# An attention and feed-forward kernel on one core: casts of sums moved to GpSimd, the sums of w2 spread over more blocks, and the weights of q and k loaded by block

## The chip, the core and the metric

The kernel runs on one core of a Trainium2 chip. The core has a matrix engine (TensorE, PE in the profile; its weight loads are PEld), three engines for elementwise work (VectorE or DVE, ScalarE or ACT, GpSimd or POOL) and SyncE (SP), whose queue issues the DMA transfers. Each engine works through its own queue in order: an instruction that waits holds up all that stand behind it on that engine. The metric is the device time in microseconds. Before the change three runs gave 889.3, 886.95 and 889.46 us, median 889.3.

## The reference

For 2048 tokens of width D = 512:

```python
xn = _layernorm(x)
q, k, v = split(xn @ wqkv)            # 32 heads of 16
scores = q k^T * 16**-0.5, kept where 0 <= i - j < 256
s = (softmax(scores) @ v) @ wo
h = silu(xn @ w1) * (xn @ w3)         # F = 1792
g = silu(h @ w2)
out = x + s * g
```

## The kernel before

**Tiles and precision.** The tokens are cut into NT = 4 blocks t of 512, and the 32 heads into four groups g. A tile (t, g) is one block of one group; two units of attention make a tile, so there are 32 units n, eight for each t. A product of two float32 matrices is made of float16 parts: each operand is cut into a high half (the cast) and a low half (what the cast left), and three matmuls are added: high by high, low by high, high by low. So every operand of a matmul costs a cast and a subtraction on one of the elementwise engines.

**What PE does in order.** The order of PE's instructions is the order in which the program makes them (only PE is in ORDERED). On the other engines a scheduler chooses the order, after dependences and priorities; the tanh and the products that free a PSUM bank are marked urgent. A unit of attention is a series of small steps: maxima of the scores (L639 on PE, L653 on DVE), scores again with the maximum taken off (L719), mask (L726, DVE), exponential (L729, ACT), values (L747), and the end of a tile (L762 to L802, normalise): sums are turned over through DRAM, `rb` is the reciprocal broadcast, POOL multiplies `on` by it, and `cut` makes the two halves of `on` for the product with wo. Between the steps the program spreads pieces of other work, each with a cost: projections of q and k (project, L583), values (L553), the feed forward (L978, L1168, L1098), and the totals (total, L1206 to L1221). `later(n, f)` puts f into a queue that is worked off n steps on, so that an elementwise step is placed in the program well before its user.

**Feed forward.** F is cut into FB = 14 blocks f. gate_up(t, f) multiplies xn by 128 columns of w1 (part k = 0, then tanh on ACT, L993, and a product on DVE, L997) and of w3 (k = 1, then L1002 on DVE). For t = 0 the blocks go into w2 by down (L1168), and the halves of w1 and w3 are stored to DRAM (dW1, L984) for t = 1 to 3, which load them ready made (L820). For t = 1 to 3 two blocks make a pair j (seven pairs), and the product with w2 is folded: seven products of sums (fold_down_piece, L1098) stand for eight of halves. The sums on the side of h are made for each t by fold_first (L1040, L1041) and fold_second (sums L1062 to L1065 on POOL, the casts L1055 on ACT, what the casts leave L1057 on POOL). The sums on the side of w2 are made once, by fold_weights(j), in t = 1 with f = 1 to 7: two raw blocks are loaded (L931), scaled (L940, ACT), summed (L925, POOL), cast (L948, ACT), subtracted (L950, POOL) and stored to DRAM (dW2, L955); load_fold (L1079) reads them. At the end of a t, unfold (L1132 and the helper halves, L327) makes four accumulators from the seven products on POOL, 14 additions, and total makes silu of each, multiplies it into the product of the attention with wo (L1212) and adds x. The last total of all goes by columns (L1234 to L1245).

**Slots.** Nearly all these tiles live in 47 slots of 2 KB in each partition. `take` gives the one that has been free longest; `give(x, after=n)` returns it n steps later. A new tile waits on the chip until the last reader of the old tile in that slot is done.

**Weights of q and k.** `weights_qk's cut` makes float16 halves of a group's weights (whi, wlo: eight tiles that stay in SBUF for the whole kernel), which project uses for every t.

## Time and profile before

| | |
|---|---|
| runs | 889.3, 886.95, 889.46 us (median 889.3) |
| profiled execution, its own time | 890.93 us |
| its span | 889.2 us |
| mean granted TensorE clock | 0.969 |
| PE busy | 812.9 us (91%) |
| DVE, ACT, POOL busy | 629.3, 434.3, 384.1 us |

The profile tells of one execution. The span is the time from the first to the last instruction, in microseconds; the profiled execution's own time lies 1.7 us above it. "PE 812.9 (91%)" is the busy time and its share of the span. A line of a timeline has the start, the duration, the engine, the source line, the operation and its tiles (out<-in), how many were put together (x9), and in brackets the idle time of the engine ahead of it with the instruction that ended the idle time ("<-ACT pt L729": ACT's line 729, which wrote tile pt). A line of a group gives the busy time of all and the mean in nanoseconds of one, then the idle time ahead of them and what ended it. A table of stretches has for each stretch the busy time of PE, PEld, DVE, ACT and POOL with their counts, the granted clock, the busy share of the DMA and its GB/s.

### The profile page before, as it was taken

Reading aid. Unit: us, or ns where it says so; the run is one execution under the profiler, and the core shown is the slowest. Engines: PE = TensorE matmul, PEld = TensorE weight load, DVE = VectorE, ACT = ScalarE, POOL = GpSimd, SP = SyncE. Lnnn points to the kernel's source line nnn. Section 1 sums busy time; section 2 is a strip of 40 time slices with the busy share of each in tenths; the row PEclk is TensorE's granted clock in tenths of the full one; section 3 lists DMA queues with packets and bytes.
Section 4 is the critical chain, followed back from the end, with each engine's and each line's share of the span. In section 5 each row is a group of like instructions: output and inputs, shape, how many; then the busy total and the mean of one; then the engine's idle time right before and its main releaser. Section 6 shows DMA issues by size and latency. Waiting matters only on the chain.

```text
span 889.2 us, 24220 instructions
## 1 busy us (share of the span) xinstructions
PE 812.9 (91%) x9302; PEld 424.7 (48%) x9302; DVE 629.3 (71%) x2013; ACT 434.3 (49%) x655; POOL 384.1 (43%) x621
## 2 busy tenths in 40 slices
PE   8999988999889669999999999999999998989995
PEld 4444444444434234654446544466445543457472
DVE  8787886788767438757878788866777776664444
ACT  6899773636365545434443344444444243444511
POOL 2257353524278786113351635310434453441653
PEclk9999999999989779999999999999999998999997
DMA  9978354353465466743543454554444641443321
GB/s 284 267 246 253 114 150 117 114 144 96 121 171 140 149 186 161 219 133 104 173 118 101 137 139 127 140 161 114 126 102 116 184 112 39 118 138 117 110 54 48
DMA packets 113812, 125.42 MB, mean 141 GB/s; under 512 B 18656, under 2 KB 76320, under 8 KB 113696
## 3 DMA queue, kind: packets, MB, share of 16 engines
q1 hardware_dynamic: 113408, 123.35, 49.0%
q8 instruction: 73, 1.20, 0.6%
q10 hardware_dynamic: 288, 0.52, 0.2%
q14 instruction: 43, 0.35, 0.1%
HBM read 88.21 MB, written 31.33 MB: 134 GB/s over the span
## 4 chain that ended last, share of the span: by engine, by line
PE 53%; DVE 12%; POOL 11%; ACT 10%; DMA 6%; issue 5%; SPq 2%; ACTq 0%; POOLq 0%; DVEq 0%
PE m L978 17%; PE m L1098 8%; PE po L747 7%; PE m L1212 5%; PE m L583 4%; DVE junk L653 3%; PE s L719 3%; PE m L553 3%; DMA slot<-in_B_w_dram 3%; POOL slot L327 3%; ACT pt L729 2%; ACT slot L330 2%; POOL slot L1057 2%; PE s L639 2%; DVE s L726 2%
## 5 line engine op out<-in xcount | busy, mean ns | idle before, releaser
L978 PE MATMUL m<-XH,slot 128*128 128x512 f16 x896 | 272.8, 387 | 17.5 <-DVE slot L997 13.6
L729 ACT ACTIVATE pt<-s,es 128x1024 f32<-128x1024 f32 x152 | 167.3, 1110 | 152.7 <-DVE s L726 145.3
L978 PEld LDWEIGHTS <-slot 128*128 128x128 f16 x1344 | 126.3, 99 | 178.0 <-issue 38.1
L327 POOL TENSOR_TENSOR slot<-slot,slot 128x256 f16<-128x256 f32 (+1 forms) x162 | 108.2, 695 | 195.5 <-ACT slot L1011 60.5
L978 PE MATMUL m<-XL,slot 128*128 128x512 f16 x448 | 172.3, 385 | 0.0
L726 DVE TENSOR_TENSOR s<-s,MK 128x256 f32<-128x256 f32 (+2 forms) x280 | 119.3, 435 | 60.0 <-PE s L719 57.7
L653 DVE CUSTOM_DVE_ANT_0 junk<-s,MW 128x320 bf16<-128x320 f32 x276 | 134.0, 485 | 25.4 <-PE s L639 17.1
L1098 PE MATMUL m<-slot,slot 128*128 128x256 f16 x882 | 102.5, 273 | 1.4 <-DVE slot L596 1.1
L1098 PEld LDWEIGHTS <-slot 128*128 128x128 f16 x882 | 84.5, 98 | 18.2 <-issue 4.6
L653 DVE CUSTOM_DVE_ANT_0 junk<-po,MW 128x320 bf16<-128x320 f32 x172 | 83.6, 486 | 5.8 <-DVE mt L678 0.6
L1057 POOL TENSOR_TENSOR slot<-slot,slot 128x256 f16<-128x256 f32 x126 | 82.0, 679 | 0.0
L719 PE MATMUL s<-qa,KA 50*64 50x320 f16 (+3 forms) x1472 | 60.6, 263 | 22.9 <-ACT pt L729 18.6
L997 DVE SCALAR_TENSOR_TENSOR slot<-slot,m 128x512 f32<-128x512 f32 x56 | 38.4, 685 | 58.7 <-ACT slot L993 57.5
L747 PE MATMUL po<-pt,V 64*32 64x320 f32 (+4 forms) x2880 | 78.7, 347 | 0.0
L1055 ACT CAST slot<-slot 128x512 f16<-128x512 f32 x63 | 38.9, 617 | 64.1 <-DVE slot L1002 31.8
L719 PEld LDWEIGHTS <-KA 50*64 50x64 f16 x1472 | 32.0, 106 | 74.8 <-issue 52.7
L747 PEld LDWEIGHTS po<-pt,V 64*32 64x32 f32 x2880 | 52.0, 107 | 21.6 <-issue 1.5
L1062 POOL TENSOR_TENSOR slot<-slot,slot 128x256 f32<-128x256 f32 x21 | 15.3, 727 | 99.2 <-DVE slot L1002 99.2
L639 PE MATMUL s<-KA,qa 48*64 48x320 f16 (+3 forms) x824 | 46.2, 297 | 12.1 <-ACT pt L729 10.8
L1212 PE MATMUL m<-slot,slot 128*128 128x512 f16 x180 | 47.8, 415 | 7.9 <-ACT slot L801 7.3
L993 ACT ACTIVATE slot<-m,sgs 128x512 f32<-128x512 f32 x56 | 38.2, 682 | 28.2 <-PE m L978 28.2
L327 POOL TENSOR_TENSOR on<-on,rb 128x256 f32<-128x256 f32 x32 | 23.1, 741 | 59.3 <-DMA rb<-de 59.2
(184 smaller groups left out, 1212.4 us busy)
## 6 DMA issues: line engine op xcount, KB each, us to landing
slot<-dW SPq DMA_DIRECT2D x147, 256.0 KB
slot<-in_B_w_dram SPq DMA_DIRECT2D x56, 256.0 KB
slot<-in_A_x_dram SPq DMA_DIRECT2D x30, 256.0 KB
dW<-slot SPq DMA_DIRECT2D x28, 256.0 KB
KA<-dK SPq DMA_DIRECT2D x24, 288.0 KB
dW<-slot SPq DMA_DIRECT2D x49, 128.0 KB
qa<-dQ SPq DMA_DIRECT2D x32, 192.0 KB
dQ<-slot SPq DMA_DIRECT2D x16, 256.0 KB
```

What stands on the lines that cost most here:

```text
L327: op(out[:, c], a[:, c], b[:, c])
L639: nc.tensor.matmul(s[c:c + w, r, :n], qa[rows, 2 * p + a, ii * P + c:ii * P + c + w], ka[rows, 2 * p + a, e - n:e], start=True, stop=True)
L653: lasts["maximum"] = nc.vector.tensor_tensor_reduce(out=junk[:, :n], in0=s[:, r, :n], in1=mask, scale=1.0, scalar=NEG, op0=ALU.add, op1=AL ...
L719: nc.tensor.matmul(s[64 * h:64 * h + 64, r, o:o + 64 * n], ka[rows, 2 * p + a, 64 * (m + 4):64 * (m + 5)], qa[rows, 2 * p + a, 64 * (m + k ...
L726: nc.vector.tensor_add(v, v, MK[:, kind, of:of + n, :].unsqueeze(1).to_broadcast([P, 2 * len(which), n, 64]))
L729: nc.scalar.activation(pt, s, AF.Exp, scale=es)
L747: nc.tensor.matmul(cell["po"][32 * i:32 * i + 32, h, 64 * (m + k):64 * (m + k + n)], V[64 * h:64 * h + 64, (4 * t + m // 2) % VB, hd * VW: ...
L978: nc.tensor.matmul(cell[k], w[:, (a * NC + c) * P:(a * NC + c + 1) * P], b[:, c, :], start=c == 0 and i == 0, stop=c == NC - 1 and i == 2)
L1055: nc.scalar.copy(hi, view)
L1057: sub(lo[:, k], view[:, k], hi[:, k])
L1098: nc.tensor.matmul(ps, made[:, f:f + P], wj[:, 256 * b:256 * b + 256], start=j == j0 and n == 0, stop=j == j1 - 1 and n == 2)
L1212: nc.tensor.matmul(ps, O[t, g][:, a, tb], w[g], start=g == 0 and i == 0, stop=g == NG - 1 and i == 2)
```

## The change

1. **Slots and weights of q and k.** SLOTS goes from 47 to 55. The eight constant tiles of q's and k's weights are gone: cut writes both halves of one of them into a slot (WQ[t, g, k]); after t = 0's projection the slot is stored to DRAM (dWQ, eight stores of 256 KB, eight steps later) and given back; for t = 1 to 3 load_qk loads it again at the end of the unit before its use (24 loads of 256 KB).
2. **fold_weights in three parts.** The pairs are loaded with blocks f of FOLD_AT, their sums are made with block f + 1, and the four cuts come 6, 8, 10 and 12 steps after that block's second piece. The slots of the raw sums are returned 6 steps later rather than 4.
3. **fold_second.** The casts of the two sums (not of o itself) are made by GpSimd, in two halves each, ahead of each subtraction; these two cuts come 2 and 4 steps later rather than 1 and 2.
4. **normalise.** The cast of `on` is made by GpSimd in two halves rather than by ACT.
5. **unfold.** For the last t the 14 additions are made by VectorE.
6. **Stores of dW1** come 8 steps later rather than 2.

```diff
@@ -52,3 +52,3 @@
 VB = 10
-SLOTS = 47
+SLOTS = 55
 ORDERED = {ENGINE.PE}
@@ -56,2 +56,3 @@
 FOLDS = ((0, 4), (4, 7))
+FOLD_AT = (0, 1, 2, 4, 6, 8, 10)
 SEVEN = (0, 1, 3, 4, 5, 6, 2)
@@ -223,2 +224,3 @@
     dK = [dram.tile([P, TERMS, S], F16, name=f"dK{g}") for g in range(NG)]
+    dWQ = dram.tile([NG, 2, P, 2 * D], F16, name="dWQ")
     dW1 = dram.tile([FB, 2, P, 2 * NC * P], F16, name="dW1")
@@ -334,3 +336,4 @@
 
-    WQK = {}
+    WQ = {}
+    ES = {}
     SQ = {}
@@ -392,9 +395,6 @@
         def cut(ks=(1, 0)):
-            if "hi" not in cell:
-                cell["hi"] = const.tile([P, 2, NC, P], F16, name=f"whi{g}")
-                cell["lo"] = const.tile([P, 2, NC, P], F16, name=f"wlo{g}")
-            hi, lo = cell["hi"], cell["lo"]
             for k in ks:
                 raw = cell["raw"][k]
-                split(hi[:, k].rearrange("p c f -> p (c f)"), lo[:, k].rearrange("p c f -> p (c f)"), raw, cell["sw"])
+                WQ[0, g, k] = both = take(F16)
+                split(both[:, 0:D], both[:, D:], raw, cell["sw"])
                 give(raw)
@@ -405,3 +405,3 @@
             nc.vector.tensor_scalar(es, cell["p2"], cell["p2"], DH**-0.5 / QS**2, op0=ALU.mult, op1=ALU.mult)
-            WQK[g] = hi, lo, es
+            ES[g] = es
         return load, norm, scale, cut
@@ -576,3 +576,3 @@
             assert turned[t] == 4
-            hi, lo, _ = WQK[g]
+            w = WQ[t, g, k]
             xh, xl = X[t]
@@ -581,4 +581,4 @@
             for c, i in parts[n]:
-                a, b = ((hi, xh), (lo, xh), (hi, xl))[i]
-                nc.tensor.matmul(cell["pp"], a[:, k, c, :], b[:, c, :], start=(c, i) == parts[0][0],
+                a, b = ((0, xh), (1, xh), (0, xl))[i]
+                nc.tensor.matmul(cell["pp"], w[:, (a * NC + c) * P:(a * NC + c + 1) * P], b[:, c, :], start=(c, i) == parts[0][0],
                                  stop=(c, i) == parts[-1][-1])
@@ -586,2 +586,9 @@
                 return
+            if t == 0:
+                def store():
+                    nc.sync.dma_start(dWQ[g, k], w)
+                    give(w, after=4)
+                later(8, store)
+            else:
+                give(w)
             pp = cell["pp"]
@@ -607,2 +614,6 @@
 
+    def load_qk(t, g, k):
+        WQ[t, g, k] = w = take(F16)
+        nc.sync.dma_start(w, dWQ[g, k])
+
     def fetch(t, g):
@@ -699,3 +710,3 @@
 
-        es = WQK[g][2]
+        es = ES[g]
         cell = {}
@@ -800,3 +811,4 @@
             O[t, g] = o = made.rearrange("p (a q) -> p a q", a=2)
-            nc.scalar.copy(o[:, 0, :], on)
+            for c in (slice(0, 256), slice(256, 512)):
+                nc.gpsimd.tensor_copy(o[:, 0, c], on[:, c])
             halves(nc.gpsimd.tensor_sub, o[:, 1, :], on, o[:, 0, :])
@@ -921,16 +933,12 @@
 
-    def pool_parts(op, *calls):
-
-        for out, a, b in calls:
-            op(out, a, b)
-
     def fold_weights(j):
 
-        raws = [take(F32) for _ in range(2)]
-        for i, raw in enumerate(raws):
-            nc.sync.dma_start(raw, w2[(2 * j + i) * P:(2 * j + i + 1) * P, :])
-        e, o = raws
+        cell = {}
         l, r = slice(0, 256), slice(256, 512)
         sub = nc.gpsimd.tensor_sub
-        cell = {}
+
+        def load():
+            cell["raw"] = [take(F32) for _ in range(2)]
+            for i, raw in enumerate(cell["raw"]):
+                nc.sync.dma_start(raw, w2[(2 * j + i) * P:(2 * j + i + 1) * P, :])
 
@@ -938,7 +946,10 @@
             assert folded
-            for i, raw in enumerate(raws):
+            e, o = cell["raw"]
+            for i, raw in enumerate((e, o)):
                 nc.scalar.activation(raw, raw, AF.Copy, scale=fold_w[:, 2 * j + i:2 * j + i + 1])
             cell["z"] = z, y = [take(F32) for _ in range(2)]
-            pool_parts(sub, (z[:, l], e[:, r], e[:, l]), (z[:, r], o[:, r], z[:, l]),
-                       (y[:, l], o[:, r], e[:, r]), (y[:, r], o[:, l], z[:, r]))
+            sub(z[:, l], e[:, r], e[:, l])
+            sub(z[:, r], o[:, r], z[:, l])
+            sub(y[:, l], o[:, r], e[:, r])
+            sub(y[:, r], o[:, l], z[:, r])
 
@@ -950,3 +961,3 @@
                 sub(a[:, n + c:n + c + 256], raw[:, c:c + 256], a[:, c:c + 256])
-            give(raw, after=4)
+            give(raw, after=6)
 
@@ -958,7 +969,9 @@
             later(4, store)
-        later(4, sums)
-        later(6, lambda: cut(e, 256, (0,)))
-        later(7, lambda: cut(o, 512, (1, 2)))
-        later(9, lambda: cut(cell["z"][0], 512, (4, 5)))
-        later(11, lambda: cut(cell["z"][1], 512, (6, 3)))
+
+        def cuts():
+            e, o = cell["raw"]
+            z, y = cell["z"]
+            for n, work in enumerate(((e, 256, (0,)), (o, 512, (1, 2)), (z, 512, (4, 5)), (y, 512, (6, 3)))):
+                later(2 * n, lambda work=work: cut(*work))
+        return load, sums, cuts
 
@@ -985,3 +998,3 @@
                     give(w, after=4)
-                later(2, store)
+                later(8, store)
             else:
@@ -1054,4 +1067,7 @@
             hi, lo = (made[:, 512 * k:512 * k + 512].rearrange("p (e c q) -> p e c q", e=2, c=2) for k in range(2))
-            nc.scalar.copy(hi, view)
+            if raw is o:
+                nc.scalar.copy(hi, view)
             for k in range(2):
+                if raw is not o:
+                    nc.gpsimd.tensor_copy(hi[:, k], view[:, k])
                 sub(lo[:, k], view[:, k], hi[:, k])
@@ -1066,4 +1082,4 @@
         cut(o, oo, (1, 3), (e,))
-        later(1, lambda: cut(sums[0], z, (4, 5)))
-        later(2, lambda: cut(sums[1], y, (6, 2)))
+        later(2, lambda: cut(sums[0], z, (4, 5)))
+        later(4, lambda: cut(sums[1], y, (6, 2)))
 
@@ -1124,3 +1140,3 @@
         q = [QS7.pop((t, i)) for i in range(7)]
-        add = nc.gpsimd.tensor_add
+        add = nc.gpsimd.tensor_add if t < NT - 1 else nc.vector.tensor_add
         for b in range(4):
@@ -1251,2 +1267,3 @@
         late = []
+        cuts_at = []
         for t in range(NT):
@@ -1271,4 +1288,9 @@
 
-                    if t == 1 and 1 <= f <= FB // 2:
-                        pieces.append((0, lambda f=f: fold_weights(f - 1)))
+                    if t == 1 and f in FOLD_AT:
+                        work = fold_weights(FOLD_AT.index(f))
+                        pieces.append((0, work[0]))
+                        cuts_at.append((f + 1, work))
+                    for at, work in cuts_at:
+                        if t == 1 and f == at:
+                            pieces.append((0, work[1]))
                 if f == FB - 4 and t + 2 < NT:
@@ -1278,3 +1300,7 @@
                     pieces += soon
-                pieces += gate_up(t, f)
+                made = gate_up(t, f)
+                for at, work in cuts_at:
+                    if t == 1 and f == at:
+                        made.insert(2, (0, lambda work=work: later(6, work[2])))
+                pieces += made
                 pieces += late
@@ -1485,2 +1511,3 @@
     beside = [[] for _ in units]
+    ahead = [[] for _ in units]
     for n in range(len(units)):
@@ -1488,6 +1515,7 @@
         for k in range(3, len(tiles)):
-            if max(2 * k - 5 + (k == NG), 0) == n:
-                beside[n] += project(*tiles[k], 1)
-            if 2 * k - 4 == n:
-                beside[n] += project(*tiles[k], 0)
+            for u, half in ((max(2 * k - 5 + (k == NG), 0), 1), (2 * k - 4, 0)):
+                if u == n:
+                    beside[n] += project(*tiles[k], half)
+                if u == n + 1 and tiles[k][0]:
+                    ahead[n].append((0, lambda k=k, half=half: load_qk(*tiles[k], half)))
         if n % 8 >= 4 and t < NT - 1:
@@ -1496,2 +1524,3 @@
             beside[n] += [(0, lambda t=t, b=n % 8 - 2: residual(t - 1, b))] + total(t - 1, n % 8 - 2)
+        beside[n] += ahead[n]
     other = [sum(c for c, _ in b) for b in beside]
```

## The prediction

> **What bounds the kernel now.** I read the head of the page first, then stretches of 25 us, then each idle time of TensorE (PE) of over half a microsecond, then on ScalarE (ACT) and GpSimd (POOL) what was late.
>
> ```profile
> span 889.2 us, 24220 instructions
> PE 812.9 (91%) x9302; PEld 424.7 (48%) x9302; DVE 629.3 (71%) x2013; ACT 434.3 (49%) x655; POOL 384.1 (43%) x621
> DMA packets 113812, 125.42 MB, mean 141 GB/s; under 512 B 18656, under 2 KB 76320, under 8 KB 113696
> ```
>
> PE is busy for 91%, and its order is fixed by the program. So the kernel shortens only where PE sits idle or runs at half clock. No other engine is full over the span, but the stretches differ (columns: start:end, length, busy us of each engine with its count, granted clock, DMA share, GB/s):
>
> ```profile
> 50.00:75.00 25.00, 23.50 (x186) 10.54 (x186) 20.08 (x79) 24.91 (x53) 16.10 (x26) 1.00 0.80 257
> 225.00:250.00 25.00, 21.03 (x274) 10.34 (x263) 20.30 (x66) 8.45 (x12) 9.20 (x14) 0.93 0.41 111
> 250.00:275.00 25.00, 20.73 (x233) 9.76 (x232) 14.86 (x51) 17.27 (x29) 21.72 (x34) 0.86 0.55 153
> 275.00:300.00 25.00, 17.62 (x225) 8.18 (x223) 12.61 (x37) 12.32 (x19) 20.88 (x33) 0.85 0.48 133
> 300.00:325.00 25.00, 16.57 (x120) 7.05 (x119) 9.51 (x32) 11.88 (x19) 19.04 (x30) 0.81 0.57 170
> 325.00:350.00 25.00, 23.59 (x290) 11.75 (x289) 18.93 (x57) 14.23 (x21) 15.84 (x25) 0.93 0.68 193
> 850.00:889.00 39.00, 27.88 (x190) 18.71 (x187) 17.80 (x24) 4.99 (x8) 19.55 (x27) 0.87 0.18 52
> ```
>
> From 225 to 350 PE is busy for 99.5 of 125 us, at clocks of 0.81 to 0.93. That is the stage in which w2's seven sums are made (fold_weights, seven times), and POOL is nearly full in its middle. The tail loses 11 us more. PE's idle times of that stage, of the later blocks and of the tail:
>
> ```profile
> 236.66 0.41 PE L719 MATMUL s<-qa,KA 50*64 50x320 f16 x9 [3.97 <-ACT pt L729]
> 263.60 1.01 PE L978 MATMUL m<-XH,slot 128*128 128x512 f16 x2 [4.27 <-DVE slot L997]
> 268.62 0.60 PE L978 MATMUL m<-XH,slot 128*128 128x512 f16 x2
> 297.79 1.01 PE L978 MATMUL m<-XH,slot 128*128 128x512 f16 x2 [7.38 <-DVE slot L997]
> 315.61 0.64 PE L719 MATMUL s<-qa,KA 50*64 50x320 f16 x12 [5.77 <-ACT pt L729]
> 324.78 0.33 PE L639 MATMUL s<-KA,qa 48*32 48x320 f16 x8 [2.65 <-ACT pt L729]
> 344.87 0.42 PE L719 MATMUL s<-qa,KA 50*64 50x320 f16 x11 [0.74 <-ACT pt L729]
> 437.08 0.42 PE L719 MATMUL s<-qa,KA 50*64 50x320 f16 x11 [2.07 <-ACT pt L729]
> 741.74 0.97 PE L719 MATMUL s<-qa,KA 50*64 50x320 f16 x24 [1.81 <-ACT pt L729]
> 743.95 0.48 PE L639 MATMUL po<-KA,qa 48*64 48x320 f16 x4 [1.23 <-DVE M L653]
> 842.77 0.59 PE L978 MATMUL m<-XH,slot 128*128 128x512 f16 x2 [1.03 <-DVE slot L997]
> 874.06 8.70 PE L1212 MATMUL m<-slot,slot 128*128 128x512 f16 x27 [7.31 <-ACT slot L801]
> ```
>
> After 263.60 two matmuls take 1.01 us, from 268.62 on 0.60: five microseconds after a long idle time run at some half speed, which costs about 2.4 us besides. I charge 2.4 us to each idle time of 4 us or more.
>
> Each of these waits ends at ACT, so the question is what held ACT. Ahead of 297.79 (ACT's timeline, then VectorE's, DVE):
>
> ```profile
> 291.41 0.62 ACT L1055 CAST slot<-slot 128x512 f16<-128x512 f32 x1 [1.49 <-POOL slot L1063]
> 293.97 0.62 ACT L948 CAST slot<-slot 128x512 f16<-128x512 f32 x1 [0.63 <-POOL slot L1057]
> 295.22 1.14 ACT L948 CAST slot<-slot 128x512 f16<-128x512 f32 x2 [0.63 <-POOL slot L1057]
> 296.26 0.68 ACT L993 ACTIVATE slot<-m,sgs 128x512 f32<-128x512 f32 x1
> ```
>
> ```profile
> 297.05 0.69 DVE L997 SCALAR_TENSOR_TENSOR slot<-slot,m 128x512 f32<-128x512 f32 x1 [8.65 <-ACT slot L993]
> ```
>
> The tanh (L993) that releases PE waits for nothing itself; it stands in ACT's queue behind casts whose inputs are sums that POOL has not made, or whose target slots POOL's subtractions still read. POOL is the resource of this stage, and ACT's first-in first-out queue carries its lateness to PE.
>
> **The change, part by part.** Prices of one instruction come from these groups:
>
> ```profile
> L1055 ACT CAST slot<-slot 128x512 f16<-128x512 f32 x63 | 38.9, 617 | 64.1 <-DVE slot L1002 31.8 <-POOL slot L1063 22.0 <-POOL slot L1065 10.1
> L801 ACT CAST slot<-on 128x512 f16<-128x512 f32 x16 | 9.9, 618 | 39.4 <-POOL on L327 36.6 <-DMA slot<-dW 2.8
> L1057 POOL TENSOR_TENSOR slot<-slot,slot 128x256 f16<-128x256 f32 x126 | 82.0, 679 | 0.0
> L1063 POOL TENSOR_TENSOR slot<-slot,slot 128x256 f32<-128x256 f32 x21 | 15.3, 729 | 1.4
> L1412 POOL MEMSET KA<- 128x384 f32 x4 | 1.5, 412 | 0.0
> L1244 DVE TENSOR_TENSOR slot<-slot,slot 128x256 f32<-128x256 f32 x2 | 0.8, 424 | 0.1
> ```
>
> POOL takes 84 half casts from fold_second (2 × 42 of the 63 casts of L1055) and 32 from normalise (2 × 16 of L801). The trace has no such copy. The memset of 384 columns at 0.412 us scales to 0.28 for 256 columns, the least; a two-input subtraction, 0.68, is the most. I take 0.42: one input, but it reads, so it lies between and nearer the memset. 116 × 0.42 = 49 us more on POOL (32 to 79), less 14 sums at 0.73 that leave: 384 becomes about 423 us. ACT loses 42 × 0.62 + 16 × 0.62 = 36 us. Neither total matters by itself; where they lie does.
>
> *w2's sums spread, casts off ACT.* Load, sums and cuts of the seven pairs go to blocks 0, 1, 2, 4, 6, 8, 10 and the blocks after. By the changed program's order, the stretch in which PE does what it did at 250 to 350 holds some 70 us of POOL work (added casts counted) against 82 before, and later stretches take the rest. Its first wait: at 229.27 the raw loads were issued, held behind a store,
>
> ```profile
> 221.94 0.35 SPq L955 DMA_DIRECT2D dW<-slot  x1
> 229.27 1.33 SPq L931 DMA_DIRECT2D slot<-in_B_w_dram  x3
> ```
>
> so ACT's scaling of them came late and PE stood at 236.66. Now the load stands a block ahead of the sums and that store comes later in SP's queue: −3.97 −2.4 = −6.4. At 263.60 the tanh now stands ahead of the casts of w2 that held it: −4.27 −2.4 = −6.7. The three from 315 to 345 were casts of L1055 waiting for L1063, now on POOL, and of a pair that is moved later: −5.77 −2.65 −0.74 −2.4 = −11.6.
>
> The wait of 297.79 does not go. In the new order, POOL gets from the place of 264.5 up to the sum that the last cast ahead of this tanh needs, some 52 instructions in a row: 9 copies × 0.42 + 15 sums × 0.73 + 27 subtractions × 0.68 = 33 us. It could start at 264.5, ends at 297.6 on before's clock; cast, tanh and product (0.62 + 0.68 + 0.69) bring PE to 299.6, while PE would be there at 297.79 − 7.38 = 290.4. So 9.2 us, and with short waits for DVE in between some 11.4, in place of 7.4: +4. Later, where two more pairs meet (the place of 404 to 413), a cast waits behind 8 us of POOL work with some 6 us of slack in ACT's queue: +2. Sum of the stage: −6.4 −6.7 −11.6 +4 +2 = −18.7. Bounds: all waits and half clocks gone, −34.5; copies at 0.68 and two stalls come back, +8.
>
> *Other blocks from t = 1 on.* 437.08, 741.74, 743.95 and 842.77 hold 2.07 + 1.81 + 1.23 + 1.03 = 6.1 us of waits, the first two and the last of the same kind. POOL's order there now does cast and subtraction in one go, and the later steps (2 and 4 for 1 and 2) leave the sums time. I take −5 (−9, if half as much again lies in shorter waits; or +3, if POOL, now fuller, delivers operands late).
>
> *Weights of q and k by block.* 8 stores and 24 loads of 256 KB more on SP, 32 issues at the 0.44 us of the three raw loads above = 14 us of SP's queue, and 8 MB on top of the 125 MB that the DMA moves. By the order each load stands at least 20 us of PE work ahead of its use. Nothing on the path; if that cover were gone, each of the 24 would be a wait like that of 236.66.
>
> *Later stores of w1 and w3* (8 steps for 2) and *55 slots*. In t = 0 SP now issues the loads of w1 and w3 at places some 4 us later against PE, and ACT is full there (24.91 of 25 at 50 to 75). PE has few waits there now. I take +2 for the stage (−3 with more slots free; +8 if half of the 14 blocks lose 1.1 us).
>
> *The tail.* The last unfold's 14 sums leave POOL for DVE:
>
> ```profile
> 858.34 3.78 SPq L795 DMA_DIRECT2D rb<-de  x8
> 867.87 1.86 POOL L327 TENSOR_TENSOR slot<-slot,slot 128x256 f32<-128x256 f32 x2
> 871.50 1.85 POOL L327 TENSOR_TENSOR on<-on,rb 128x256 f32<-128x256 f32 x2
> 873.39 0.62 ACT L801 CAST slot<-on 128x512 f16<-128x512 f32 x1 [1.18 <-POOL on L327]
> 867.92 2.35 DVE L1207 SCALAR_TENSOR_TENSOR slot<-slot,slot 128x512 f32<-128x512 f32 x2 [2.32 <-ACT slot L1206]
> ```
>
> The product with rb need no longer wait behind them. rb has landed by about 864 (its issues end at 862.1; I allow 2 us): two products 1.5, two copies 0.84, two subtractions 1.4, so PE may go on at 867.8 rather than 874.06: −6.2, and −2.4 as the idle time no longer reaches 4 us. DVE's remaining 8 sums × 0.42 end about 869, then the four products with tanh; it becomes the last, which gives some of that back: −7 (−4 to −8).
>
> Sum: −18.7 −5 +2 −7 = −28.7 against this execution's own 890.93, which is 1.6 above the median of 889.3: 862.
>
> **A rule against the change.** POOL's two sums at 867.87 took 1.86 us, where 2 × 0.73 would be 1.46, while DVE ran two L1207. The Trainium skill, "GPSIMD Engine Reference", section "1. Specifications", says that GpSimd shares its SBUF interfaces with VectorE and contends with DVE instructions that read two SBUF inputs. By that rule the casts belong on ACT; this row agrees. If every moved half cast were stretched by 1.86/1.46 as that row is, POOL gets 49 × 0.27 = 13 us more, a quarter of it in the crowded stage, so the sum would be near −25.
>
> **The rivals.** *POOL becomes the bound.* A copy costs 0.68 and the bunch at 264 to 287 has 9 × 0.26 = 2.3 us more, the stalls of 315 to 345 stay behind it (11.6 not gained), and the other blocks give nothing (5): 862 + 2.3 + 11.6 + 5 = 881. For it: POOL at 21 of 25 us already. Against: 12 us leave the stretch.
>
> *The stage is freed.* POOL's work shares out so that 297.79 goes too: −34.5 −5 +2 −7 gives 846. For it: less work than before; against: the 33 us in a row.
>
> *Slower: t = 0's loads of w1 and w3 come late.* The mechanism is SP's queue: stores of dW1 and dWQ and the loads of w1, w3 in one order, the latter issued 4 us later, at a DMA share of 0.80, and ACT with no slack to catch up. If each of the 14 blocks waits 3 us for its weights, +42 in place of +2: 862 + 40 = 902. It decides from 28.7 + 2 = 31 us, 2.2 us a block. Against: PE has 23.50 of 25 us there, and the loads still lead their use by 3.6 us and more.
>
> **How the numbers follow.** Forecast case (850 to 874) 0.50; freed (below 850) 0.10; POOL the bound (874 to 886.6) 0.18; within 0.3% of the median, about what the measurement can tell, 0.05; slower 0.17. So faster 0.78. The range: from the freed case's 846, less 1, to 892, with 0.17 above and 0.03 below; the forecast's own is 850 to 874.
>
> **What would show it.** PE's waits near 236 and 263 gone; one of 9 to 12 us on DVE's L1010 (L997 before) at some 285 to 300, with POOL full for 30 us ahead of it and ACT's cast of w2 before the tanh; no wait over 1 us where 315 to 345 was; POOL copies at 0.28 to 0.68; the last wait under 4 us. It is wrong if blocks of t = 0 wait for w1's loads, or if new waits on POOL stand in t = 2 and 3.

## The result and the profile after

The changed kernel takes 858.79 us (median of 856.75 to 859.68) against 889.38 for the kernel before: a ratio of 0.9651, with a 95% interval of 0.9616 to 0.9686. The forecast was 862. The head of the page of the changed kernel:

```profile
span 857.9 us, 24287 instructions
PE 804.5 (94%) x9302; PEld 420.7 (49%) x9302; DVE 635.0 (74%) x2027; ACT 402.1 (47%) x597; POOL 416.1 (49%) x723
```

POOL is 32 us busier and ACT 32 us less busy. PE's busy time fell by 8 us though its work is the same: fewer matmuls ran at half clock, and the mean granted clock rose from 0.969 to 0.982. The stage of w2's sums, in the same columns as before:

```profile
225.00:250.00 25.00, 23.23 (x306) 11.46 (x303) 22.57 (x73) 10.53 (x16) 15.19 (x25) 1.00 0.43 131
250.00:275.00 25.00, 22.92 (x274) 11.19 (x267) 16.37 (x50) 15.46 (x26) 20.35 (x34) 0.93 0.57 166
275.00:300.00 25.00, 13.97 (x180) 6.33 (x179) 10.28 (x31) 9.02 (x14) 24.62 (x41) 0.80 0.46 128
300.00:325.00 25.00, 24.86 (x275) 11.62 (x274) 20.13 (x64) 11.66 (x15) 9.16 (x16) 1.00 0.79 218
325.00:350.00 25.00, 25.00 (x325) 15.01 (x322) 19.49 (x65) 11.59 (x15) 15.14 (x25) 1.00 0.46 138
```

PE is busy for 110.0 us of the 125, where it was 99.5. What is left of the loss stands in one stretch, 275 to 300, in which POOL has 24.62 of 25 us. PE's waits of over 1.8 us from 200 to 600, and those of the tail:

```profile
265.43 0.41 PE L650 MATMUL po<-KA,qa 48*64 48x320 f16 x4 [1.89 <-DVE M L664]
296.12 1.01 PE L583 MATMUL m<-XH,slot 128*128 128x512 f16 x2 [11.03 <-DVE slot L1010]
398.10 0.42 PE L730 MATMUL s<-qa,KA 50*64 50x320 f16 x11 [2.34 <-ACT pt L740]
483.04 0.41 PE L730 MATMUL s<-qa,KA 50*64 50x320 f16 x8 [2.26 <-ACT pt L740]
537.82 0.59 PE L991 MATMUL m<-XH,slot 128*128 128x512 f16 x2 [2.09 <-DVE slot L1010]
845.09 2.98 PE L1228 MATMUL m<-slot,slot 128*128 128x512 f16 x13 [0.66 <-POOL slot L329]
848.71 2.75 PE L1228 MATMUL m<-slot,slot 128*128 128x512 f16 x12 [0.64 <-DVE slot L1232]
```

The waits of 236, 263, 315 and 324 are gone (the one of 265.43 is another's), that of 297 is longer (7.38 before), and the tail's 7.31 became two of 0.66 and 0.64.

PE's order is the same in all these kernels but for one piece, so each matmul of one trace can be lined up with the same matmul of another. The table has how far each kernel's profiled execution is behind (+) or ahead (−) of the kernel before's, at the place where the kernel before was at the time at the head of the column. It is worked out from the two traces and shows where time is won or lost. Each trace is one execution, and runs of one kernel differ by several us (e2_spread's from 880.9 to 891.2), so a difference of 2 or 3 us between two rows may be chance. The last column but one is the median of the runs, the last its ratio to the runs of the kernel before on the same chip. That kernel's median was 889.3 to 892.2 us from chip to chip, so two medians of different rows are comparable to some 2 us; the ratio is free of this.

| kernel | 225 | 350 | 425 | 575 | 650 | 775 | 850 | 875 | median | ratio [95%] |
|---|---|---|---|---|---|---|---|---|---|---|
| changed | +0.9 | −15.9 | −13.8 | −8.9 | −8.9 | −20.3 | −24.0 | −30.4 | 858.8 | 0.965 [0.962, 0.969] |
| e1_unfold | −0.8 | 0.0 | −1.2 | −2.0 | −2.0 | −5.6 | −3.8 | −7.6 | 885.8 | 0.994 [0.990, 0.999] |
| e2_spread | −0.4 | −8.3 | −4.0 | −0.3 | +0.2 | −2.3 | −0.4 | −0.4 | 886.6 | 0.996 [0.993, 0.999] |
| e3_casts | +1.5 | +9.4 | +7.3 | +5.3 | +5.7 | −0.9 | −1.6 | −0.6 | 889.0 | 0.997 [0.995, 1.000] |
| e4_slots | −0.2 | +5.2 | +4.6 | +6.6 | +6.4 | −0.2 | −2.7 | −2.7 | 886.8 | 0.996 [0.994, 0.998] |
| a1_casts_act | −0.1 | −14.2 | −14.2 | −4.0 | −4.0 | −10.0 | −12.4 | −19.7 | 870.0 | 0.976 [0.975, 0.978] |
| a5_nospread | +2.0 | +6.8 | +9.2 | +13.1 | +13.2 | +1.7 | −2.0 | −8.6 | 879.8 | 0.987 [0.984, 0.990] |
| a6_noslots | +2.4 | +1.0 | +3.4 | +0.9 | +1.0 | −5.8 | −4.3 | −10.6 | 879.2 | 0.986 [0.985, 0.988] |
| a7_s47 | +1.5 | −0.7 | +9.8 | +9.6 | +9.5 | +1.4 | +3.4 | −2.9 | 887.9 | 0.998 [0.996, 1.001] |
| a2_give8 | +3.4 | −10.4 | −6.5 | −3.0 | −3.2 | −11.7 | −15.4 | −22.0 | 867.3 | 0.976 [0.972, 0.979] |
| a3_w2_dve | +0.8 | −15.4 | −16.6 | −9.0 | −8.9 | −20.3 | −24.0 | −30.2 | 861.0 | 0.967 [0.964, 0.970] |
| a9_w2low_dve | +1.1 | −12.2 | −8.1 | −6.6 | −6.6 | −18.0 | −21.7 | −28.3 | 864.0 | 0.970 [0.965, 0.975] |
| a13_clear_queue | +0.7 | −7.2 | −7.7 | −1.0 | −0.9 | −14.0 | −17.7 | −23.9 | 869.3 | 0.976 [0.972, 0.980] |

Names with e are the kernel before with one part of the change, names with a the changed kernel with one thing undone or another one added.

### The profile page after: what moved, and what is told of

It is laid out like the page before. It is cut to its first block, busy times and chain, and to the rows that moved or that the text cites. A ratio compares the mean times of both kernels' runs of the same rounds, so it can differ in the third digit from the quotient of the medians.

```text
span 857.9 us, 24287 instructions
## 1 busy us (share of the span) xinstructions
PE 804.5 (94%) x9302; PEld 420.7 (49%) x9302; DVE 635.0 (74%) x2027; ACT 402.1 (47%) x597; POOL 416.1 (49%) x723
## 4 chain that ended last, share of the span: by engine, by line
PE 56%; DVE 14%; POOL 11%; DMA 6%; ACT 5%; issue 4%; SPq 2%; POOLq 0%; ACTq 0%; DVEq 0%
PE m L991 21%; PE m L1114 10%; PE po L758 6%; PE m L583 5%; DVE junk L664 4%; PE m L1228 4%; PE s L730 4%; DMA slot<-in_B_w_dram 3%; POOL slot L329 3%; PE m L553 2%; POOL slot L1073 2%; PE s L650 2%; PE m L1184 2%; DVE s L737 2%; ACT pt L740 1%
## 5 line engine op out<-in xcount | busy, mean ns | idle before, releaser
L991 PE MATMUL m<-XH,slot 128*128 128x512 f16 x896 | 272.9, 387 | 7.5 <-DVE slot L603 4.5
L991 PEld LDWEIGHTS <-slot 128*128 128x128 f16 x1344 | 126.2, 99 | 166.8 <-issue 28.3
L329 POOL TENSOR_TENSOR slot<-slot,slot 128x256 f16<-128x256 f32 (+1 forms) x156 | 104.2, 697 | 146.0 <-ACT slot L1024 68.2
L1114 PEld LDWEIGHTS <-slot 128*128 128x128 f16 x882 | 84.4, 98 | 19.1 <-issue 5.1
L583 PE MATMUL m<-XH,slot 128*128 128x512 f16 x240 | 72.4, 386 | 12.8 <-DVE slot L1010 12.8
L1073 POOL TENSOR_TENSOR slot<-slot,slot 128x256 f16<-128x256 f32 x126 | 82.7, 676 | 0.6
L583 PEld LDWEIGHTS <-slot 128*128 128x128 f16 x384 | 36.1, 99 | 56.7 <-issue 17.4
L1006 ACT ACTIVATE slot<-m,sgs 128x512 f32<-128x512 f32 x56 | 38.2, 682 | 37.9 <-PE m L991 37.8
```

What stands on the lines that cost most here:

```text
L329: op(out[:, c], a[:, c], b[:, c])
L583: nc.tensor.matmul(cell["pp"], w[:, (a * NC + c) * P:(a * NC + c + 1) * P], b[:, c, :], start=(c, i) == parts[0][0], stop=(c, i) == parts[ ...
L991: nc.tensor.matmul(cell[k], w[:, (a * NC + c) * P:(a * NC + c + 1) * P], b[:, c, :], start=c == 0 and i == 0, stop=c == NC - 1 and i == 2)
L1073: sub(lo[:, k], view[:, k], hi[:, k])
L1114: nc.tensor.matmul(ps, made[:, f:f + P], wj[:, 256 * b:256 * b + 256], start=j == j0 and n == 0, stop=j == j1 - 1 and n == 2)
```

## The experiments

**One part alone.** Four kernels took one part each.

e1_unfold, the last unfold on VectorE:

```diff
-        add = nc.gpsimd.tensor_add
+        add = nc.gpsimd.tensor_add if t < NT - 1 else nc.vector.tensor_add
```

> The kernel before with one part of the change: the last unfold's 14 additions on VectorE. If the tail gains because GpSimd no longer holds the product with rb back, as predicted: 4 to 8 us less than before, nothing moved ahead of 850 us, and the last wait of TensorE, 7.3 us before, under 2 us. Rival: the tail only follows from what happened ahead of it (GpSimd's backlog of the last folds), and the addition on VectorE delays the products with tanh there: under 2 us gained.

The median fell by 4.8 us, within what the first theory gave. The trace has 3.8 us of its 7.6 behind 850; the rest had wandered in before, which this edit doesn't touch. PE's last wait is 3.51 us, not under 2. So the edit alone is worth about 4 us in the tail, and the changed kernel gains about 7 there (−24.0 at 850, −31.3 at the end of the span). Three kernels that keep both this edit and the casts of `on` on GpSimd, and each lack another part, gain as much there (a1_casts_act 8.5, a5_nospread 7.3, a6_noslots 7.5), which points to those casts; no run has them alone.

e2_spread, fold_weights in three parts (the same code as in the change):

```diff
+FOLD_AT = (0, 1, 2, 4, 6, 8, 10)
...
+                    if t == 1 and f in FOLD_AT:
+                        work = fold_weights(FOLD_AT.index(f))
```

> The kernel before with fold_weights in three parts at blocks 0, 1, 2, 4, 6, 8, 10 and nothing else. If the stage from 225 to 350 us is limited by w2's sums coming together on GpSimd: 8 to 17 us less, the wait at 236 gone, the stage's later waits (315 to 345) mostly gone, one long wait left near 290. Rival: the waits of ScalarE's casts in fold_second on GpSimd carry the stage, and spreading w2 alone leaves them: under 5 us less, with L1055's waits for L1063 as before (22 us) and waits over 2 us at 315 to 345.

The stage gives 7.9 us and the wait at 236 is gone, as the theory had it, but by 500 us the gain is lost again. The median is 4.0 us less, which is on the rival's side (under 5), and the rival's sign came too: ACT's casts in fold_second waited 20.0 us in all for POOL's sums, nearly the 22.0 of before. The waits that come new are of the same kind at new places. In that kernel the stretches from 400 to 475 read as follows; before, the granted clock was 1.00 in all three.

```profile
400.00:425.00 25.00, 23.19 (x259) 10.51 (x258) 17.76 (x55) 12.01 (x17) 14.39 (x22) 0.93 0.44 127
425.00:450.00 25.00, 22.92 (x266) 10.76 (x265) 19.79 (x66) 10.77 (x15) 12.24 (x25) 1.00 0.54 150
450.00:475.00 25.00, 22.54 (x287) 12.35 (x286) 17.13 (x50) 8.47 (x12) 7.14 (x11) 0.86 0.47 132
```

e3_casts, the casts of fold_second's two sums on GpSimd (and the two cuts 2 and 4 steps later, as in the change):

```diff
-            nc.scalar.copy(hi, view)
+            if raw is o:
+                nc.scalar.copy(hi, view)
             for k in range(2):
+                if raw is not o:
+                    nc.gpsimd.tensor_copy(hi[:, k], view[:, k])
```

> The kernel before with the casts of fold_second's two sums on GpSimd (84 half casts, cuts at 2 and 4 steps) and nothing else. By the prediction's reading GpSimd is nearly full from 250 to 328 us and gets some 8 us more there, so ScalarE's gain and GpSimd's lateness about cancel in that stage, and the later blocks give 3 to 6 us: 0 to 8 us less in all. Rival one: ScalarE's waits in the first-in first-out queue are the whole cause: 12 us less or more. Rival two: GpSimd becomes the bound: 3 us slower or more, with a wait over 12 us near 290 to 300.

In all 1.6 us less, as expected; but by parts, 7.9 us lost in the stage and 7.3 won from 650 to 850. In the stage of w2's sums, without the spread, the casts on POOL cost time; later they do not.

e4_slots, 55 slots, weights of q and k by block, stores of dW1 later:

```diff
-SLOTS = 47
+SLOTS = 55
...
-                later(2, store)
+                later(8, store)
```

> The kernel before with 55 slots, weights of q and k by block, and the stores of dW1 eight steps later; all casts, sums and w2 as before. By the prediction nothing of it is on the path but t = 0's loads: between 3 us less and 5 us more, all of it ahead of 225 us. Rival: reused slots hold work up all over the kernel, and eight more of them carry a good part of the gain: 8 us less or more, spread over t = 1 to 3.

3.8 us less in the median. The trace lost 5.4 in the stage and won 9.1 from 650 to 850, which the first expectation did not have; the rival's 8 us or more did not come either.

The four gains add to 4.8 + 4.0 + 1.6 + 3.8 = 14 us, each of them uncertain by 2 to 4; the whole change gave 30.6. (The casts of `on` were not run alone.) So about half of the gain is there only when the parts stand together.

**One part undone.** a1_casts_act gives the casts of e3_casts back to ACT in the changed kernel (the cuts stay 2 and 4 steps later):

> The changed kernel with the casts of fold_second's two sums back on ScalarE (all else kept). In the kernel before, these casts on GpSimd alone cost 8 us in the stage of w2's sums and gave 8 us later. Theory: with w2 spread GpSimd has room, so the casts are worth something in both stretches: 8 to 16 us slower than the changed kernel (867 to 875), with waits of ScalarE's casts for GpSimd's sums back at 300 to 350 and in t = 3. Rival: only the later blocks profit: 8 us slower, all of it behind 650 us. Rival: the gain is that of the spread and the order the scheduler happens to choose: within 4 us.

870.0: 11 us slower, as the theory had it. But the loss is not in the stage (−14.2 at 350 against −15.9), and PE's waits at 300 to 350 did not come back; it comes between 425 and 575 (5 us against the changed kernel) and from 650 to 850 (7).

a5_nospread puts fold_weights back as it was:

> The changed kernel with fold_weights as before the change (seven blocks in a row, f = 1 to 7; all else kept). Theory: without the spread GpSimd is full from 250 to 330 us and the added casts make it worse, as they did alone: 18 to 28 us slower than the changed kernel (877 to 887), all of it between 225 and 350 us. Rival: the spread is worth what it gave alone, 0 to 5 us, as the 8 us that it gave in the stage came back at 450 to 500.

879.8: 21 us slower, all of it between 225 and 350 (22.7 by 350 in the table). So w2's sums, made in a row, are what this stage cannot take when the rest is changed.

a6_noslots is the changed kernel with 47 slots, constant weights of q and k, and early stores:

```diff
-SLOTS = 55
+SLOTS = 47
...
-                later(8, store)
+                later(2, store)
```

> The changed kernel without 55 slots, without weights of q and k by block, and with the stores of dW1 two steps later as before (w2 spread, casts and last unfold as changed). As predicted these are not on the path: within 4 us of the changed kernel (855 to 863). Rival: with the casts later and raw sums held longer 47 slots are too few, and new tiles wait for old readers: 8 us slower or more, with waits of DMA or ScalarE for slots in t = 1 to 3.

The expectation failed and its rival came: 879.2, 20 us slower, 15.4 of it between 225 and 350. What is left (the spread, the casts, the last unfold) is still 12 us faster than the kernel before. a7_s47 then changed the number of slots alone:

```diff
-SLOTS = 55
+SLOTS = 47
```

> The changed kernel with SLOTS 47 instead of 55 and nothing else undone (weights of q and k by block, later stores, spread, casts all kept). Without all three of these parts the changed kernel took 879. If the number of slots is what they bring (in t = 1's first blocks a slot is taken again within 4 steps of its return with 47, within 9 with 55): 872 to 886, with ScalarE's scaling of w2 waiting for the raw loads' DMA, or SP for slots, between 250 and 350 us. Rival: the later stores, which take SP's queue out of the way of the loads, or the weights by block bring it: within 5 us of the changed kernel.

887.9, 2 us above the expected range, which can't be told from the kernel before (ratio 0.998, 0.996 to 1.001). This kernel is poorer in memory than the one before: the eight constant tiles, 2 KB each in a partition, became the eight added slots, and a7_s47 has neither. With 47 slots that also hold the weights of q and k, the rest of the change gives nothing; with 47 slots beside constant weights and early stores (a6_noslots) it gives 12 us. The later stores and the weights by block were not undone one at a time. A wait of a7_s47, and the group of the same line in the changed kernel:

```profile
ACT slot L949 <- DMA slot<-in_B_w_dram: 26.8, 7, 8.2
```

```profile
L949 ACT ACTIVATE slot<-slot,fw 128x512 f32<-128x512 f32 x14 | 9.7, 717 | 6.4 <-DMA slot<-in_B_w_dram 6.4
```

ACT waits 26.8 us for w2's raw blocks instead of 6.4, 18.6 of it between 225 and 350: a load is issued later, as it needs a slot whose old readers are done, and so do other loads ahead of it in SP's queue (which of the two held a given load, the trace does not name). Counted in the program: in t = 1's first blocks a slot is taken again a median of 4 steps after its return with 47 slots, and 9 with 55; a step is some 1.33 us (857.9 us over 643 steps).

**The wait that stayed.** Four kernels went for the 11.03 us before 296.12. ACT's timeline of the changed kernel ahead of it:

```profile
287.74 1.45 ACT L959 CAST slot<-slot 128x256 f16<-128x256 f32 x3 [9.01 <-POOL slot L1073]
291.58 0.40 ACT L959 CAST slot<-slot 128x256 f16<-128x256 f32 x1 [2.39 <-POOL slot L961]
291.89 0.72 ACT L949 ACTIVATE slot<-slot,fw 128x512 f32<-128x512 f32 x1
294.14 0.62 ACT L959 CAST slot<-slot 128x512 f16<-128x512 f32 x1 [1.54 <-POOL slot L952]
294.67 0.68 ACT L1006 ACTIVATE slot<-m,sgs 128x512 f32<-128x512 f32 x1
```

The tanh (L1006) stands behind casts of w2. The prediction took the sum (L952) to be what holds it; 9.01 us of the wait name a subtraction of fold_second (L1073), which does not feed that cast. By the order of the program the cast writes into the slot of the sum that this subtraction still reads. SP's queue was held there too, at a raw load of w2 (its waits from 225 to 430):

```profile
SPq L943 <- POOL slot L1073: 8.1, 1, 8.1
```

a3_w2_dve took the sums away from GpSimd:

```diff
-            sub(z[:, l], e[:, r], e[:, l])
+            nc.vector.tensor_sub(z[:, l], e[:, r], e[:, l])
```

(and the other three likewise).

> The changed kernel with w2's 28 half sums on VectorE instead of GpSimd (0.42 for 0.73 us each). If the wait of 11 us before 296 is the row of GpSimd work ahead of the sum that ScalarE's cast needs: eight of those sums leave the row, 5.8 us, and the cast no longer needs GpSimd's sum at all: that wait 1 to 6 us, and 5 to 12 us faster than the changed kernel (847 to 854). Rival: the tanh is held by the slots that GpSimd's subtractions still read, or VectorE's queue now waits for ScalarE's scaling and holds the masks: that wait stays over 8 us, and the time within 3 us or slower.

The wait stayed at 9.70 and the time at 861.0, a ratio of 0.967 that can't be told from the changed kernel's 0.965. The sum that the cast needs, now on VectorE, waited for ACT's scaling (DVE's timeline):

```profile
292.84 1.07 DVE L952 TENSOR_TENSOR slot<-slot,slot 128x256 f32<-128x256 f32 x1 [8.09 <-ACT slot L949]
```

That scaling stands in ACT's queue behind the cast of w2 that waits for the slot (7.59 us here). So the sums on GpSimd are not what holds most of it: 1.3 of 11.0 us went with them.

a2_give8 gave that slot back later:

```diff
-            give(raw, *give_too, after=4)
+            give(raw, *give_too, after=8)
```

> The changed kernel with the slots of fold_second's sums returned 8 steps after their cut instead of 4. In the changed kernel the wait of 9 us of ScalarE's cast of w2 ahead of TensorE's 11 us names a GpSimd subtraction of fold_second, and by the order this cast writes into the slot of the very sum that the subtraction reads. Theory: the wait is that of slot reuse; the cast now gets a slot whose readers are long done, TensorE's wait near 296 falls to 5 us or less, and the kernel takes 846 to 854. Rival: the row of 33 us on GpSimd ahead of the sum that a later cast needs, as the prediction has it, holds the tanh by itself: that wait 8 us or more, and the time within 3 us of the changed kernel.

The cast no longer waits there. SP's queue does now: a load for the feed forward (L832) waited 6.0 us for POOL's L1072, a cast of fold_second, the raw load of w2 stands behind it, and ACT's scaling waits for that load:

```profile
293.43 0.72 ACT L949 ACTIVATE slot<-slot,fw 128x512 f32<-128x512 f32 x1 [7.70 <-DMA slot<-in_B_w_dram]
```

PE's wait is 9.53 us and the kernel 867.3, 8 us slower than the changed one: neither the theory nor the rival, which had the time within 3 us.

a9_w2low_dve took 49 subtractions off GpSimd:

```diff
-            for c in range(0, n, 256):
-                sub(a[:, n + c:n + c + 256], raw[:, c:c + 256], a[:, c:c + 256])
+            nc.vector.tensor_sub(a[:, n:2 * n], raw[:, 0:n], a[:, 0:n])
```

> The changed kernel with what w2's casts leave taken by VectorE in one instruction per cut (28 of 128x256 or 128x512) instead of 49 on GpSimd. Taking away one slot conflict (a2_give8) or the sums (a3_w2_dve) left TensorE's wait of 9.5 us near 296: each time GpSimd's row let go of a slot or an input about 288, and another user waited for it. If that row is the cause, whichever tile it holds, then 12 of its subtractions (8 us) are gone and the wait falls to 1 to 5 us; VectorE takes 7 us more in the stage beside some 10 of 25 us busy: 846 to 855. Rival one: VectorE's queue now waits for ScalarE's casts and holds masks and products: the wait goes elsewhere, 858 or slower. Rival two: the raw loads of w2 behind SP's queue are what is late: the wait stays over 8 us with ScalarE's scaling waiting for DMA.

864.0, and the wait is 9.75. POOL now idles ahead of it, and yet the same cast waits for the same subtraction (POOL's timeline, then ACT's):

```profile
275.70 0.84 POOL L1079 TENSOR_TENSOR slot<-slot 128x256 f32<-128x256 f32 x1 [5.29 <-DVE slot L1014]
```

```profile
292.28 1.23 ACT L959 CAST slot<-slot 128x256 f16<-128x256 f32 x3 [8.82 <-POOL slot L1072]
```

So it is not a backlog of 30 us either (this kernel's lines from there on are one less: its L1072 is L1073). The last part of fold_second's own series for this pair (three sums, three casts and five subtractions, with two products and a cast of normalise between them) takes POOL from 283.58 to 292.2, and the cast of w2 hangs on its end.

a13_clear_queue moved w2's casts to GpSimd and the third pair a block on, so that nothing of w2 stands ahead of that tanh on ACT:

```diff
-FOLD_AT = (0, 1, 2, 4, 6, 8, 10)
+FOLD_AT = (0, 1, 3, 4, 6, 8, 10)
...
-            nc.scalar.copy(a[:, 0:n], raw[:, 0:n])
             for c in range(0, n, 256):
+                nc.gpsimd.tensor_copy(a[:, c:c + 256], raw[:, c:c + 256])
```

> The changed kernel with w2's casts also made by GpSimd (49 halves, 20 us more there) and the third and fourth pair of w2 a block apart from the second (FOLD_AT 0, 1, 3, 4, 6, 8, 10). By the order of the program, ScalarE now has nothing of w2 between the cast of a fold's last block and the tanh that held TensorE for 9.5 to 11 us in the changed kernel and in three variants of it. Theory: the tanh only waits because it stands in ScalarE's queue behind work of w2 whose inputs or slots depend on GpSimd, each time another piece of it: the wait near 296 falls under 2 us, and the kernel takes 843 to 851, although GpSimd has 20 us more. Rival: GpSimd itself is the bound, and with 20 us more slots and operands come later: new waits of 4 us or more between 260 and 420 us, 857 or slower.

The wait grew to 14.77 and the time to 869.3. Something else now stands ahead of the tanh, the tanh of total for the block before, whose result goes into a slot that POOL's subtraction of w2 (L961) still reads, and POOL has 24.84 of 25 us there:

```profile
297.90 0.63 ACT L1222 ACTIVATE slot<-slot 128x512 f32<-128x512 f32 x1 [17.25 <-POOL slot L961]
298.43 0.67 ACT L1006 ACTIVATE slot<-m,sgs 128x512 f32<-128x512 f32 x1
```

```profile
275.00:300.00 25.00, 12.53 (x206) 6.24 (x205) 9.45 (x24) 4.70 (x6) 24.84 (x47) 0.83 0.44 125
```

What these four share: at this place some instruction ahead of the tanh, on ACT or on SP, needs a slot or an input that POOL releases at 288 to 298. Which one it is differs each time. That it would end with more slots, or with the tanh ahead of all work that uses just returned slots, is not shown: no run had more than 55 slots, and none set the tanh ahead of all of it. None of these kernels beats the changed one.

## Why the prediction came out

**The time was right (862 against 858.8), and so were the largest waits and all its signs but one: two new waits on POOL stand in t = 2 (483.04 and 537.82).** That the sum came so close is in part luck: the stage gave 4.0 us less than its term, and the other blocks 5.2 more. By its terms:

- *The stage, 225 to 425: −18.7 forecast, −14.7 found* (+0.9 to −13.8 in the table). The waits of 236, 263 and 315 to 345 went as forecast. The stall that stays was forecast at 11.4 us and measured 11.03; the later one, forecast at 2, measured 2.34 at 398.10. By the two traces PE's idle time fell by 10.1 us there (the forecast's waits come to 11.4) and its busy time by 4.7, where three charges of 2.4 for half clock, 7.2 in all, had been expected to go. What the forecast lacks is the wait of 265.43, and half clock behind it and behind 398.10.
- *Other blocks: −5 forecast, −10.2 found* (−13.8 at 425, −24.0 at 850). It is a sum of two things: 5 us lost by 575, and 15 won from 650 to 850. The gain is larger than the term because the list of waits behind it was too short: it has 4.1 us in that stretch, while PE idled for 15.1 us there before (among it 2.34 at 792.28 and 1.93 at 709.92) and for 4.3 in the changed kernel; 4.5 us of busy time went besides. (e1_unfold, whose edit does not reach this stretch, shows 1.8 us there, so that much may be chance.) The loss is the bound that the prediction named, POOL delivering late, and half clock after the two new waits. Ahead of 483.04 ACT's tanh of total waited 10.80 us for POOL's additions of unfold (L1148), with the exponential that PE needs behind it; ahead of 537.82 it waits for POOL again, with the tanh that PE needs behind it:

```profile
535.81 0.63 ACT L1222 ACTIVATE slot<-slot 128x512 f32<-128x512 f32 x1 [4.12 <-POOL slot L1073]
536.35 0.67 ACT L1006 ACTIVATE slot<-m,sgs 128x512 f32<-128x512 f32 x1
```

- *t = 0: +2 forecast, +0.9 found.* SP's later loads, the place of the rival on the slow side, cost no more than executions differ there (−0.8 to +3.4 in the table's column).
- *Tail: −7 forecast, −7.3 found* (−24.0 at 850 to the span's −31.3).
- *The price of a cast on GpSimd: 0.42 taken, 0.40 measured*, near the memset's end of the bounds:

```profile
L1072 POOL CAST slot<-slot 128x256 f16<-128x256 f32 x84 | 32.5, 401 | 21.0 <-issue 9.4 <-PE m L1228 5.4 <-PE m L1114 5.2
```


**Where it was wrong: the slots.** The prediction put 55 slots with the later stores, at +2 (−3 to +8) and in t = 0 alone, and the weights by block as "nothing on the path". The runs show the opposite: without these three parts the changed kernel loses 20 us (a6_noslots), with 47 slots and the weights in them 29 (a7_s47), and nearly all of that arises from 225 on. What failed is that each edit was priced as a term of a sum; but the terms hang together, as the spread gives 4 us alone and costs 21 when it alone is missing. The reading that fits the waits is that GpSimd's added casts keep each slot longer, that the spread lets raw sums live a block longer, and that both only pay if the next user does not get a slot that GpSimd still reads; no run takes these steps one by one. Why the sum came out all the same is not shown; most likely because it was made from the order of the whole changed program, in which the slots already were.

**The step on the stall** named the right place, size and engine, but for the most part the wrong tie: the cast ahead of the tanh does wait for the sum that POOL makes for w2, but for 1.54 us, while 9.01 us are POOL's release of a slot. a3_w2_dve, which takes that sum from POOL, shortened PE's wait from 11.03 to 9.70 and not the time. That 11.4 came so near to 11.03 is luck in part: 2.2 of it are short waits for DVE that the prediction did not work out.

**The rule on shared interfaces.** In the changed kernel's tail two products on POOL took 1.59 us while DVE was adding (L1148, from 841.34 to 843.51); two of the same took 1.42 us at 281.79 (POOL's timeline, below). DVE's three additions there took 2.17 us, where two of its half additions at 838.70, with POOL idle, took 0.76:

```profile
281.79 1.42 POOL L329 TENSOR_TENSOR on<-on,rb 128x256 f32<-128x256 f32 x2
...
841.64 1.59 POOL L329 TENSOR_TENSOR on<-on,rb 128x256 f32<-128x256 f32 x2 [7.59 <-DMA rb<-de]
```

Over the whole kernel little of it shows: POOL's subtractions took 676 ns in the mean (L1073) against 679 before (L1057), and DVE's busy time rose by 5.7 us, while its 14 new additions alone took 8.0 (0.58 to 0.64 us each, where the prediction had taken 0.42):

```profile
L1148 DVE TENSOR_TENSOR slot<-slot,slot 128x256 f32<-128x256 f32 x8 | 4.8, 636 | 0.1
L329 DVE TENSOR_TENSOR slot<-slot,slot 128x256 f32<-128x256 f32 x6 | 3.2, 576 | 0.1
```

The contention that the Trainium skill states ("GPSIMD Engine Reference", section "1. Specifications") is visible where POOL and DVE stand side by side in the tail, as in the prediction's row, but it did not make the moved casts a loss: undoing them (a1_casts_act) costs 11 us.

## What to carry to other kernels

An instruction in a first-in first-out queue waits for its slot as well as for its input: before a step is moved to a busy engine, ask which tile gets the slot that this engine will now release later, and what stands behind that tile's first writer. Where work is spread out and buffers are added in one change, try each part undone as well as alone: four parts gave 14 us alone, and the change gave 31. When a wait stays though its named cause is taken away, read again which tile the releaser wrote or read; the name in the profile may be that of the slot's last reader and not of a producer.

## What the runs showed of the hardware

How long PE idles does not tell by itself whether half clock follows, nor when it sets in. After 3.42 us in a9_w2low_dve the first two matmuls took 1.01 us. After 3.14 us in a2_give8 they took 0.59, and no half clock followed; nor did it after 3.56 us in a3_w2_dve, where six took 1.45:

```profile
272.16 1.01 PE L990 MATMUL m<-XH,slot 128*128 128x512 f16 x2 [3.42 <-DVE slot L1009]
```

```profile
280.37 0.59 PE L991 MATMUL m<-XH,slot 128*128 128x512 f16 x2 [3.14 <-DVE slot L1010]
```

```profile
141.80 1.45 PE L1184 MATMUL m<-slot,slot 128*128 128x512 f16 x6 [3.56 <-DVE slot L1201]
```

After 4.51 us in e1_unfold the first two still took 0.59, but two of the same from 264.37 on took 0.98. And in the changed kernel three waits of 2.34, 2.26 and 2.09 us (398.10, 483.04, 537.82) were each followed, 0.6 to 1.0 us after PE went on, by a stretch of 3.41 us at a granted clock of 0.50 (PE's timeline of e1_unfold, then three stretches of the changed kernel):

```profile
263.73 0.59 PE L978 MATMUL m<-XH,slot 128*128 128x512 f16 x2 [4.51 <-DMA on<-os]
264.37 0.98 PE L978 MATMUL m<-XH,slot 128*128 128x512 f16 x2
```

```profile
398.68:402.08 3.40, 3.40 (x9) 1.19 (x9) 1.55 (x6) 2.00 (x2) 2.61 (x4) 0.50 0.38 118
484.01:487.42 3.41, 3.41 (x10) 1.18 (x9) 3.10 (x12) 1.13 (x2) 0.00 (x0) 0.50 0.52 177
538.63:542.03 3.40, 3.40 (x9) 1.03 (x7) 2.45 (x9) 1.60 (x2) 0.00 (x0) 0.50 0.47 140
```

At a clock of 0.50 PE does half of its work, so such a stretch costs some 1.7 us (an estimate from these rows). The prediction's charge of 2.4 us for each idle time of 4 us or more is thus too much for the 4.51 us of e1_unfold (one such stretch, from 264.45 to 267.85) and leaves out shorter waits: between 425 and 575 PE's busy time rose by 2.8 us for the same work. The Trainium skill ("TensorE: Matmul & The Clock Gate", "Part 1: The HAM clock gate") gives an idle window of about 3.4 us that runs free of the program. The 3.41 us of these stretches, and that waits of nearly one length have different ends, agree with it; that a wait of 2.09 us, shorter than the window, can be enough is measured here.

GpSimd's cast of 128x256 from float32 to float16 takes 0.40 us, against 0.68 for a subtraction of the same size: a cast there costs 0.80 for the 128x512 that ACT does in 0.62.
